# Reworking the tail, the layer-norm rows and the conditioning gradients of a fused backward kernel

## The chip, the cores and the metric

The kernel runs on one core of one Trainium2 chip. The metric is the device time of one execution in microseconds (us). A kernel is run several times and the median is quoted.

Engine names in the profile: PE is the tensor engine (matmuls), PEld its weight loads, DVE the vector engine, ACT the scalar engine, POOL the gpsimd engine, SP the engine that issues most transfers. A name ending in q (SPq) is the sequencer of that engine, which issues and waits. DMA stands for the transfer engines. "L900" is line 900 of the kernel's source.

## The reference

The program returns the output of one block and the gradients of eight of its inputs for a given `grad_out`. The block is a spectral filter (a 2-D FFT, a product with a complex weight, the inverse FFT) followed by a bilinear gated MLP; both are preceded by a layer norm that is scaled and shifted by a conditioning vector `c`. S = 2048 rows, D = 576, F = 4608, all in bf16.

```python
def _A_ref(x, w_r, w_i):                    # spectral filter
    X = rfft2(x.astype(float32)) * (w_r + 1j * w_i)
    return irfft2(X).astype(bfloat16)
def _B_ref(x, w_gate, w_up, w_down):        # gated MLP
    return ((x @ w_gate) * (x @ w_up)) @ w_down

mod = (silu(c) @ w_mod).reshape(1, 6, 1, D)
sa, ca, ga, sb, cb, gb = mod[:, 0], ..., mod[:, 5]
h = layernorm(x) * (1 + ca) + sa
x = x + ga * _A_ref(h, w_r, w_i)
h = layernorm(x) * (1 + cb) + sb
x = x + gb * _B_ref(h, w_gate, w_up, w_down)
# ... out, vjp = jax.vjp(f, A_x, w_r, w_i, w_gate, w_up, w_down, c, w_mod); vjp(grad_out)
```

The gradient of `w_mod` (576 x 3456) is the outer product of `silu(c)` with six gradient rows, those of sa, ca, ga, sb, cb, gb. The gradient of `c` (576 numbers) is `w_mod` times these six rows, times the slope of silu.

## The kernel before

The order of PE's instructions is the program's order. A list of closures called `fill` holds matmul work that is needed later but not now; `fill.run(2.5)` issues some 2.5 us of it where PE would otherwise wait. The phases are:

1. start and forward pass (to about 280 us);
2. the main loop over 18 weight blocks (to 1206.5 us), which the change does not touch;
3. **layer-norm rows**: the backward pass of the second layer norm, 16 groups of 128 rows, with the weight gradients of the last two blocks as filler;
4. **inverse transform**: eight frequency steps, with pieces of y = h·w_down (recomputed for the output; nine matmuls a piece) as filler;
5. **last rows**: 16 row groups of the first layer norm's backward pass, with the other y pieces as filler;
6. **tail**: the last two conditioning gradients, and the gradient of `c`.

The layer-norm rows. PE sums products over rows by diagonal blocks, and one filler in this stage takes its accumulator banks in pairs:

```python
def gwd(p, fb, b0):                       # gradient of w_down, 128 of its rows
    ... mm(bank[:, b0 + h, 0:288], sf[:, 0, fb, j, :], go[:, j, 288*h:288*h+288], j == 0, j == 15)   # L765
    ... # two DVE products read the pair of banks (L773)
def gw_block(p, w, m, so):                # gradient of w_gate / w_up
    ... mm(bank[:, st["b"], 0:256], h2p[...], sf[...], j == 0, False)   # L785, L789
    ... ac.copy(so()[:, m, :], bank[:, st["b"], 0:256])                 # L790, ACT frees the bank

for j in range(16):
    gh2_block(pl, j)                      # last product of the main loop, added to f32 acc on DVE
sring = [0, 1]                            # single banks;  gwd uses the pair (6, 7)
for j in range(16):
    load1(nx, ..., j + 2); load1(yl, ..., y_d, j + 2)     # row loads, 144 KB each
    n = nx[j]
    ts(n, n, rstd2[j], nmr2[j], MUL, ADD)                 # DVE
    ac.copy(b, acc[:, j, :])                              # f32 -> bf16 on ACT
    ln_bwd(b, n, mod[SCB], rstd2[j], gn, t2, go[:, j], gx)    # DVE products, ACT sums
    ...
    fill.run(1.5 if j else 4.0)
    diag_sums(b, n, j, 2, 3, 0, 192)      # of row j itself
    diag_sums(gx, yl[j], j, 5, 3, 64, None)
    fill.run(1.4)
    ...                                   # stage A of the transform of row j, ACT eviction
    if j == 11: ...                       # four table loads
for i in range(4): ...                    # w_down, 5.2 MB, after the rows
fill.flush()
```

The sums of a row group over its 128 rows are taken by ten matmuls whose diagonals are read at the end:

```python
def diag_sums(a, b, j, b0, b1, c1, col):
    for m, (d0, n) in enumerate(CH):      # four chunks of 128 columns and one of 64
        if col is not None:
            mm(bank[0:n, b1, col+m:col+m+1], a[:, d0:d0+n], ones[:, 0:1], ...)   # L898: sum of a
        mm(bank[:, b0, 128*m:128*m+128], a[:, d0:d0+n], b[:, d0:d0+n], ...)      # L900: diagonal = sum of a*b
        # m == 4: 64 columns, L902
```

The last rows and the tail:

```python
for j in range(17):
    if j < 16: Hs[j] = stage_bi(j, ...)
    if j:
        ...
        ln_bwd(gh, n, mod[SCA], ..., t2)
        fill.run(2.5)
        diag_sums(gh, n, jj, 6, 7, 0, 64)
    fill.run(2.5)
    if j in (3, 6, 9, 12): mod_grad(s, row)     # four of the six conditioning gradients
fill.flush()
diag_rows(6, 7, 0, mod[SCA], ...)               # read the diagonals, spread as rows
col_rows(7, 64, mod[SSA], ...)
mod_grad(SCA, ...); mod_grad(SSA, ...)          # the last two, 12 pairs of DVE instructions (L1130, L1131)
tensor_reduce(gc5, gsc); tt(gcb, gc5, dsl_col, MUL)
sp.dma_start(out_7[0, :].rearrange("(m q) -> q m", q=96), gcb[0:96, 0:6])   # L1174: 576 single elements
```

Of the kernel before, what the change touches and what calls it, by code (L numbers as in the profile page):

```python
# [10 lines left out]
FP32 = mybir.dt.float32  # L11
# [70 lines left out]
def build(ctx, tc, A_x, A_w_r, A_w_i, B_w_gate, B_w_up, B_w_down, c_in, w_mod, grad_out,  # L82
# [64 lines left out]
    sc_col, dsl_col, gbcol = small[:, 0:6], small[:, 6:12], small[:, 13:18]  # L147
    rstd1, nmr1 = small[:, 18:34], small[:, 34:50]
    rstd2, nmr2 = small[:, 50:66], small[:, 66:82]
    c_f, sig, tmp5 = small[:, 82:88], small[:, 88:94], small[:, 94:100]  # L150
    nt = small[:, 100:108]
    smallb = V(8640, [32])
    c_bf, sc_bf, gb_bf = smallb[:, 0:6], smallb[:, 6:12], smallb[:, 12:17]
# [52 lines left out]
    with tc.manual_schedule(engines={PE}):  # L206
# [11 lines left out]
        ve.memset(ones[:], 1.0)  # L218

# [28 lines left out]
        ve.tensor_copy(sc_col[q96], sc_bf[q96])  # L248
        ts(tmp5[q96], sig[q96], -1.0, 1.0, MUL, ADD)
        tt(tmp5[q96], tmp5[q96], c_f[q96], MUL)  # L250
        ts(tmp5[q96], tmp5[q96], 1.0, None, ADD)
        tt(dsl_col[q96], tmp5[q96], sig[q96], MUL)
# [13 lines left out]
        def mod_rows(s):  # L266
            bias = 1.0 if s in (SCA, SCB) else 0.0
            for h in range(2):
                b = single()
                for m in range(6):  # L270
                    mm(bank[:, b, 0:288], sc_rep[0:96, m, :], wm_t[s][0:96, m, 288 * h:288 * h + 288], m == 0, m == 5)
                dst = mod[:, s, 288 * h:288 * h + 288]
                if h == 0:
                    act(dst, bank[:, b, 0:288], ACT.Copy, bias=bias)
                elif bias:
                    ts(dst, bank[:, b, 0:288], bias, None, ADD)
                else:
                    ve.tensor_copy(dst, bank[:, b, 0:288])

# [261 lines left out]
        for jg in range(4):  # L541
            go_transposes(jg)
        fill.run(7.0)
# [234 lines left out]

        def gw_block(p, w, m, so):
# [36 lines left out]
        def grads(p, dring):  # L816

            out = []
            for fb in range(2):
                out += gwd(p, fb, dring())  # L820
# [15 lines left out]

        def gh2_block(p, j):
            b0 = dbank()
            for h in range(2):
                hs = slice(288 * h, 288 * h + 288)  # L840
                o = bank[:, b0 + h, 0:288]
                cs = slice(128 * j, 128 * j + 128)
                mm(o, xT[:, 1, 0, cs], wT[p][:, 0, 0, hs], True, False)  # L843
                mm(o, xT[:, 2, 0, cs], wT[p][:, 0, 1, hs], False, False)  # L844
                mm(o, xT[:, 1, 1, cs], wT[p][:, 1, 0, hs], False, False)  # L845
                mm(o, xT[:, 2, 1, cs], wT[p][:, 1, 1, hs], False, True)  # L846
# [4 lines left out]
            else:  # L851
                tt(dst, dst, src, ADD)  # L852

# [21 lines left out]
        for j in range(16):  # L875
            gh2_block(pl, j)
        nx_r = Ring(span(ST, 3, 1152), [D])
        yl_r = Ring(span(ST + 3456, 3, 1152), [D])
        F_r = Ring(span(ST + 6912, 3, 1152), [D])
        tb_r = Ring(span(ST + 10368, 2, 1152), [D])  # L880
        tg_r = Ring(span(ST + 12672, 2, 1152), [D])
        t2_r = Ring(span(ST + 14976, 2, 1152), [D])
        gx_r = Ring(span(ST + 17280, 2, 1152), [D])
        junk = V(ST + 19584, [D])
        s_r = Ring([8704, 8736], [8], FP32)
        sring = [0, 1]
        fill = Fill()
        for p in (pl - 1, pl):
            for c, f in grads(p, lambda: 6):
                fill.add(c, f)  # L890

# [12 lines left out]
        def ln_bwd(a, n, opc, rs, gn, t2, res, out):  # L904
            s = s_r.next()
            tt(gn[:], a[:], opc, MUL)  # L906
            act(junk[:], gn[:], ACT.Copy, accum_out=s[:, 0:1])  # L907
            tt(t2[:], gn[:], n[:], MUL)
            act(junk[:], t2[:], ACT.Copy, accum_out=s[:, 1:2])  # L909
            ts(s[:, 2:4], s[:, 0:2], rs, -1.0 / D, MUL, MUL)  # L910
            ts(gn[:], gn[:], rs, s[:, 2:3], MUL, ADD)  # L911
            ts(t2[:], n[:], s[:, 3:4], None, MUL)
            tt(gn[:], gn[:], t2[:], ADD)
            tt(out[:], gn[:], res, ADD)

        nx, yl = {}, {}

# [4 lines left out]
        for j in range(2):  # L922
            load1(nx, nx_r, x1_d, j, sp)
            load1(yl, yl_r, y_d, j, sp)
        for j in range(16):
            if j + 2 < 16:
                load1(nx, nx_r, x1_d, j + 2, sp)
                load1(yl, yl_r, y_d, j + 2, sp)
            n = nx[j]
            ts(n[:], n[:], rstd2[:, j:j + 1], nmr2[:, j:j + 1], MUL, ADD)  # L930
            b = tb_r.next()
            ac.copy(b[:], acc[:, j, :])
            gn, t2, gx, Fj = tg_r.next(), t2_r.next(), gx_r.next(), F_r.next()
            ln_bwd(b, n, mod[:, SCB, :], rstd2[:, j:j + 1], gn, t2, go[:, j, :], gx)
            sp.dma_start(gx1_d[:, j, :], gx[:])
            tt(gn[:], gx[:], mod[:, SGA, :], MUL)
            fold(Fj.unsqueeze(1), gn.unsqueeze(1), 1)
            fill.run(1.5 if j else 4.0)
            diag_sums(b, n, j, 2, 3, 0, 192)
            diag_sums(gx, yl[j], j, 5, 3, 64, None)  # L940
            fill.run(1.4)
            sbank[0] += 1
            ab = sring[sbank[0] % 2]
            for m in range(4):
                mm(bank[:, ab, 128 * m:128 * m + 128], Fj[:, FB[m]:FB[m] + 128], bdf, True, True)
            jj = j % 4
            mm(bank[0:32, 4, 128 * jj:128 * jj + 128], Fj[:, 256:288], bdf, True, True)
            mm(bank[32:64, 4, 128 * jj:128 * jj + 128], Fj[:, 544:576], bdf, True, True)
            evac_a(ac, ab, j)
            if jj == 3:  # L950
                evac_rem(ac, 4, j - 3, 4)
            if j == 11:
                sp.dma_start(TB.rearrange("p a b -> p (a b)"), tabs["TB"][:, :])
                sp.dma_start(TC.rearrange("p a b c -> p (a b c)"), tabs["TC"][:, :])
                sp.dma_start(TI.rearrange("p a b c -> p (a b c)"), tabs["TI"][:, :])
                sp.dma_start(TBI.rearrange("p a b -> p (a b)"), tabs["TBI"][:, :])
        wdr = V(ST + 21504, [2 * NP, D])
        for i in range(4):
            sp.dma_start(wdr[:, 9 * i:9 * i + 9, :], B_w_down[1152 * i:1152 * i + 1152, :].rearrange("(j f) d -> f j d", f=128))
        fill.flush()  # L960


        hl_t = [V(o, [NP, 256]) for o in (ACC + 24224 + 32, GO, GO + 9216, ST + 66048, ST + 75264)]
        hls = {}

        def load_hl(k):
            jp, half = k // 2, k % 2
            hls[k] = hl_t[k % 5]
            sp.dma_start(hls[k][:], hh_d[jp // 2, :, 18 * half:18 * half + 18, 256 * (jp % 2):256 * (jp % 2) + 256])

        for k in range(5):
            load_hl(k)
        RA, RB = ST, ST + 84480
        z_r = Ring(span(RA, 2, U), [4, FP])
        X_r = Ring(span(RA + 2 * U, 2, U), [2, 2, FP])
        W_r = Ring(span(RA + 4 * U, 2, U), [2, 2, FP])
        P1, P2 = V(RA + 6 * U, [2, 2, FP]), V(RA + 7 * U, [2, 2, FP])
        yb_r = Ring([ST + 62976, RA + 8 * U], [D])
        xo_r = Ring([ST + 64128, RA + 8 * U + 1152], [D])
        ac_r = Ring([RB], [2, FP], FP32)  # L980
# [252 lines left out]
```

## Time and profile before

The median of before is 1569.63 us over 13 runs (1564.67 to 1571.12). The profiled execution has a span of 1567.9 us.

| stage | from to (us) | length | PE waits in it |
|---|---|---|---|
| start, forward, main loop | 0 to 1206.54 | 1206.5 | mostly in the first 80 us |
| layer-norm rows | 1206.54 to 1317.22 | 110.68 | 17.0 |
| inverse transform | 1317.22 to 1423.55 | 106.33 | 6.4 |
| last rows | 1423.55 to 1532.23 | 108.68 | 1.3 |
| tail (after the last filler) | 1532.23 to 1567.9 | 35.67 | all |

The borders are read from PE's timeline: the end of the last gate/up group, the first matmul of the inverse transform, the first of the last rows, and the end of the last y piece.

The page of the profile, before. First the span and PE's busy time, then 40 equal slices of 39.2 us: a digit is PE's busy share in tenths, or the transfer engines'.

```profile
span 1567.9 us, 28400 instructions
PE 1475.7 (94%) x11245; PEld 988.2 (63%) x11268; DVE 810.5 (52%) x1800; ACT 515.2 (33%) x1017; POOL 261.9 (17%) x380
PE   7799998999999999999999999999999888999991
DMA  9665786976558548547745844764664598567931
```

PE is the bound (94%), and the slices show where it is not: the first ones, an eight at the end of the forward pass, three eights for the layer-norm rows and the start of the inverse transform, and the last slice, where it does almost nothing.

PE's waits from 1206 to 1318 us, before. Columns: the waiting line, what it waited for, us in total, number of times, the longest.

```profile
PE bank L785 <- ACT arena L790: 6.9, 8, 1.6
PE bank L765 <- DVE arena L773: 4.5, 2, 3.0
PE bank L785 <- ACT arena L811: 2.3, 1, 2.3
PE bank L900 <- DVE arena L914: 1.7, 2, 1.1
```

The first three are filler matmuls waiting for a bank that another engine has not emptied yet, 13.7 us together. The fourth is a row's sums waiting for that row's own chain on DVE.

Busy time in a stretch inside this stage, before. Columns: the stretch, its length, then busy us (and count) of PE, PEld, DVE, ACT and POOL, the granted clock, DMA share and GB/s.

```profile
1228.00:1270.00 42.00, 36.19 (x388) 29.33 (x388) 26.79 (x72) 21.83 (x53) 6.54 (x8) 1.00 0.89 226
```

None of the engines is full in this stretch: the rows are bound by waits among them.

The timeline of the tail, before. Columns: start, duration, engine, line, operation, out<-in; a bracket gives the idle time before it and what ended it.

```profile
1528.76 3.47 PE L1032 MATMUL bank<-arena 128*128 128x288 bf16 x27
...
1549.26 0.75 DVE L1131 SCALAR_TENSOR_TENSOR arena<-arena 96x576 bf16<-96x576 bf16 x1
...
1550.05 0.19 DVE L1170 TENSOR_REDUCE arena<-arena 128x6 f32<-128x36 f32 x1
1550.27 0.16 DVE L1172 TENSOR_TENSOR arena<-arena 96x6 bf16<-96x6 f32 x1
1550.46 0.32 SPq L1174 DMA_DIRECT2D out_dram<-arena  x1
```

The transfers issued between 1530 and 1568 us, before: how many, KB each, median us from issue to landing.

```profile
out_dram<-arena SPq DMA_DIRECT2D x2, 648.0 KB, 7.7
out_dram<-arena SPq DMA_DIRECT2D x3, 144.0 KB, 1.7
out_dram<-arena SPq DMA_DIRECT2D x1, 1.1 KB, 16.1
```

PE's last filler ends at 1528.76 + 3.47 = 1532.23. DVE then works until 1550.4, with only short pieces of PE and ACT beside it, and then a store of 1.1 KB takes 16.1 us, while a 144 KB store takes 1.7. No engine computes beside it. The packets in the profile, those of this store and of a 648 KB store before it, are over at 1553.5 us; from then to the landing at 1566.6 us the profile shows none. What the store waits for in these 13 us is not shown.

In the last rows, the sums of one row group are these PE lines of the timeline, before (the other eight of the ten alternate between these two kinds, the last pair with 64 columns):

```profile
1430.95 0.17 PE L898 MATMUL bank<-arena 128*128 128x1 bf16 x1
1430.98 0.22 PE L900 MATMUL bank<-arena 128*128 128x128 bf16 x1
...
1431.55 2.38 PE L1032 MATMUL bank<-arena 128*128 128x288 bf16 x18
```

From the first to the next filler matmul they hold PE for 0.60 us.

### The profile page before, as it was taken

The numbers are of one execution on the slowest core, as the hardware profiler recorded it, in microseconds if no ns is written. First come the engines' busy times: TensorE is split into PE (matmuls) and PEld (weight loads), VectorE is DVE, ScalarE is ACT, GpSimd is POOL, SyncE is SP. The second block draws the span as 40 slices with busy tenths as digits, with TensorE's granted clock in tenths as the row PEclk, the third lists the DMA queues.
The fourth block names the chain that finished last, engine by engine and source line by source line (L and its number), as shares of the span: only waits on it lengthen the run. The fifth ranks groups of instructions, "written<-read, shape, count | busy, mean of one in ns | idle before, by whom it ended". The sixth has DMA issues, their size and how long they took to land. (4 is left out here: it accounts for less than half of the span.)

```text
span 1567.9 us, 28400 instructions
## 1 busy us (share of the span) xinstructions
PE 1475.7 (94%) x11245; PEld 988.2 (63%) x11268; DVE 810.5 (52%) x1800; ACT 515.2 (33%) x1017; POOL 261.9 (17%) x380
## 2 busy tenths in 40 slices
PE   7799998999999999999999999999999888999991
PEld 4344443576677668667667766866766666676770
DVE  6424486533543443353354344335337775778864
ACT  5666675212212221221221222122033344343431
POOL 1122421212112202211211220221110110000000
PEclk9899998999999999999999999999999999999995
DMA  9665786976558548547745844764664598567931
GB/s 273 189 147 156 204 233 166 190 159 163 120 114 186 128 97 167 139 116 138 163 124 112 186 127 97 167 137 116 141 148 107 158 263 232 156 184 209 277 111 46
DMA packets 440998, 248.76 MB, mean 159 GB/s; under 512 B 318048, under 2 KB 418336, under 8 KB 440352
## 3 DMA queue, kind: packets, MB, share of 16 engines
q1 hardware_dynamic: 418256, 177.19, 50.4%
q0 software_dynamic: 22464, 69.62, 14.8%
q8 instruction: 88, 1.44, 0.4%
q14 instruction: 46, 0.38, 0.1%
q10 hardware_dynamic: 144, 0.13, 0.0%
HBM read 96.90 MB, written 74.20 MB: 109 GB/s over the span
## 5 line engine op out<-in xcount | busy, mean ns | idle before, releaser
L852 DVE TENSOR_TENSOR arena<-arena,bank 128x576 f32<-128x576 f32 x272 | 204.9, 753 | 305.2 <-PE bank L846 305.2
L740 ACT CAST arena<-bank 128x512 bf16<-128x512 f32 x144 | 84.4, 586 | 391.1 <-PE bank L730 373.6
L846 PE MATMUL bank<-arena 128*128 128x288 bf16 x576 | 164.6, 286 | 0.0
L843 PE MATMUL bank<-arena 128*128 128x288 bf16 x576 | 163.9, 285 | 0.5 <-DVE arena L850 0.2
L845 PE MATMUL bank<-arena 128*128 128x288 bf16 x576 | 164.3, 285 | 0.0
L844 PE MATMUL bank<-arena 128*128 128x288 bf16 x576 | 164.1, 285 | 0.0
L785 PE MATMUL bank<-arena 128*128 128x256 bf16 x1152 | 149.5, 273 | 9.2 <-ACT arena L790 6.9
L1032 PE MATMUL bank<-arena 128*128 128x288 bf16 x1152 | 152.4, 287 | 0.0
L765 PE MATMUL bank<-arena 128*128 128x288 bf16 x1152 | 146.7, 288 | 4.5 <-DVE arena L773 4.5
L734 PE MATMUL bank<-arena 128*128 128x512 bf16 x576 | 149.9, 383 | 1.0 <-ACT arena L740 1.0
L789 PE MATMUL bank<-arena 128*128 128x256 bf16 x1152 | 149.4, 273 | 0.0
L736 PE MATMUL bank<-arena 128*128 128x512 bf16 x576 | 148.7, 381 | 0.0
L765 PEld LDWEIGHTS <-arena 128*128 128x128 bf16 x1152 | 112.7, 98 | 36.7 <-issue 4.7
L1032 PEld LDWEIGHTS <-arena 128*128 128x128 bf16 x1152 | 110.8, 98 | 31.7 <-issue 3.2
L785 PEld LDWEIGHTS <-arena 128*128 128x128 bf16 x1152 | 111.0, 98 | 25.8 <-issue 12.8
L789 PEld LDWEIGHTS <-arena 128*128 128x128 bf16 x1152 | 111.9, 98 | 13.3
L744 DVE TENSOR_TENSOR arena<-arena 128x512 bf16<-128x512 bf16 x144 | 61.2, 425 | 107.3 <-ACT arena L740 107.3
L790 ACT CAST arena<-bank 128x256 bf16<-128x256 f32 x144 | 53.5, 371 | 184.1 <-PE bank L789 184.1
L734 PEld LDWEIGHTS <-arena 128*128 128x128 bf16 x576 | 50.6, 98 | 80.2 <-issue 33.0
L736 PEld LDWEIGHTS <-arena 128*128 128x128 bf16 x576 | 56.6, 98 | 68.7 <-issue 1.3
L741 ACT CAST arena<-bank 128x512 bf16<-128x512 f32 x144 | 84.8, 589 | 23.9 <-PE bank L736 23.3
L321 ACT CAST arena<-bank 128x1024 bf16<-128x1024 f32 x72 | 72.7, 1010 | 56.8 <-PE bank L317 29.1
(217 smaller groups left out, 2206.2 us busy)
## 6 DMA issues: line engine op xcount, KB each, us to landing
ghh_d<-arena POOLq DMA_DIRECT2D x72, 256.0 KB, 3.5
arena<-ghh_d POOLq DMA_DIRECT2D x36, 512.0 KB, 5.8
hh_d<-arena SPq DMA_DIRECT2D x36, 512.0 KB, 4.5
arena<-hh_d SPq DMA_DIRECT2D x16, 1152.0 KB, 7.4
out_dram<-arena POOLq DMA_DIRECT2D x36, 256.0 KB, 5.1
arena<-in_B_w_down_dram POOLq DMA_DIRECT2D x18, 288.0 KB, 4.2
out_dram<-arena POOLq DMA_DIRECT2D x36, 144.0 KB, 5.5
arena<-in_B_w_down_dram SPq DMA_DIRECT2D x4, 1296.0 KB, 7.8
```

The lines of the kernel that those rows point to most:

```text
L734: mm(bank[:, bg, :], w[:, m, fs], h2T[:, js, m, :], odd == 0 and m == 0, odd == 1 and m == 3)
L736: mm(bank[:, bu, :], w[:, 4 + k, fs], h2T[:, js, m, :], odd == 0 and k == 0, odd == 1 and k == 3)
L741: ac.copy(u[:], bank[:, bu, :])
L765: mm(bank[:, b0 + h, 0:288], sf[:, 0, fb, j, :], go[:, j, 288 * h:288 * h + 288], j == 0, j == 15)
L785: mm(bank[:, st["b"], 0:256], h2p[:, j, 128 * m:128 * m + 128], sf[:, 1 + w, :, j, :], j == 0, False)
L789: mm(bank[:, st["b"], 0:256], h2p[:, j, 128 * m:128 * m + 128], sf[:, 1 + w, :, j, :], False, j == 15)
L843: mm(o, xT[:, 1, 0, cs], wT[p][:, 0, 0, hs], True, False)
L844: mm(o, xT[:, 2, 0, cs], wT[p][:, 0, 1, hs], False, False)
L845: mm(o, xT[:, 1, 1, cs], wT[p][:, 1, 0, hs], False, False)
L846: mm(o, xT[:, 2, 1, cs], wT[p][:, 1, 1, hs], False, True)
L852: tt(dst, dst, src, ADD)
L1032: mm(bank[:, yb, 0:288], hl[:, fb % 18, 128 * (j % 2):128 * (j % 2) + 128], wdr[:, fb, 288 * h:288 * h + 288], fb == 0, fb == 35)
```

## The change

Its intent is to take PE's waits out of the last 360 us:

1. **Tail.** The last two conditioning rows come out of the sums directly as rows. Their part of the gradient of `c` is done by 45 one-column matmuls with a transposed load of `w_mod`. The gradient of `c` is turned into a row by five small matmuls and stored as one run of 1152 bytes.
2. **Last rows.** Ten diagonal-sum matmuls per row group become four column-sum matmuls of 64 columns. The other four conditioning gradients are done on 128 partitions.
3. **Layer-norm rows.** Five single banks rotate. The last product is written as bf16, so ACT's cast is gone. Two DVE operations of a row become ACT operations. The sums and stage A of row j are issued two rows later. Some filler is held back for the inverse transform, w_down is loaded during the rows (2.7 MB of it in row 12), and all masks come in one lump at the end.
4. **Inverse transform.** The filter's gradients are one step later, and there is more filler ahead of the last part of a step.
5. **Start.** silu(c) in the columns that parts 1 and 2 need comes from four small element-wise loads of `c`.

The diff, cut to its core:

```diff
+        po.memset(c2_bf[:], 0.0)                                   # start
+            for h in range(2):
+                po.dma_start(c2_bf[64 * h:64 * h + 64, 0:9], c_in[0, :].rearrange("(m q) -> q m", q=64))
+            po.dma_start(c2_bf[:, 9:13], ...); po.dma_start(c2_bf[0:64, 13:14], ...)
@@ layer-norm rows
-        for j in range(16):
-            gh2_block(pl, j)
-        sring = [0, 1]
+        sring = [0, 1, 4, 6, 7]
-            for c, f in grads(p, lambda: 6):
+            for c, f in grads(p):                                  # gwd_halves: single banks
+        def gh2_last(j):
+                tt(acc_b(j)[:, hs], acc[:, j, hs], bank[:, b, 0:288], ADD)      # bf16 out
-            ts(n[:], n[:], rstd2[:, j:j + 1], nmr2[:, j:j + 1], MUL, ADD)
-            ac.copy(b[:], acc[:, j, :])
+            act(n[:], n[:], ACT.Identity, bias=nmr2[:, j:j + 1], scale=rstd2[:, j:j + 1])
-            ts(gn[:], gn[:], rs, s[:, 2:3], MUL, ADD)
-            ts(t2[:], n[:], s[:, 3:4], None, MUL)
+            act(t2[:], n[:], ACT.Identity, bias=s[:, 2:3], scale=s[:, 3:4])
+            ts(gn[:], gn[:], rs, None, MUL)
+            if fill.left() > 9.0: fill.run(1.0)
+            if 2 <= j < 18: row_sums(j - 2)
+            if fill.left() > 9.0: fill.run(1.0)
+            if 2 <= j < 18: row_a(j - 2)
+            if j == 12: load_wdr(9, 28)
+            if j == 14: ...                                        # four table loads
+        load_wdr(28, 36)
@@ inverse transform
-                fill.run(4.0)
+                fill.run(5.0)
                 stage_ci(u, Y_t, SD_t, Gt)
-                gws[u] = grad_W(u, X)
@@ last rows
-                diag_sums(gh, n, jj, 6, 7, 0, 64)
+            if j: column_sums([gh, q], 6, j - 1, 64)
+        def column_sums(srcs, b, j, w):
+            for h in range(2):
+                for i, a in enumerate(srcs):
+                    mm(bank[w*i:w*i+w, b+h, 0:288], ones[:, 0:w], a[:, 288*h:288*h+288], ...)
@@ tail
-        diag_rows(...); col_rows(...); mod_grad(SCA, ...); mod_grad(SSA, ...)
-            sp.dma_start(out_7[0, :].rearrange("(m q) -> q m", q=96), gcb[0:96, 0:6])
+        fill.run(4.0)
+        ...                                                        # row -> columns, nine outer products, stores
+        fill.run(4.0)
+        for m in range(5):
+            for i in range(9):
+                mm(bank[0:n, 2, m:m + 1], wmT[:, i, 128*m:128*m+n], dmc[:, i:i + 1], i == 0, i == 8)
+        ...
+        for m in range(5):
+            mm(bank[0:1, m // 4, ...], gcb[0:n, m:m + 1], ident[0:n, 0:n], True, True)
+        ac.dma_start(out_7[0:1, :], grow[0:1, :])
```

## The prediction

> **What bounds it now.** The tensor engine, with three exceptions. The page has PE busy 1475.7 of 1567.9 us (94%), DVE 52%, ACT 33%. The table by stretches puts PE's idle time in three places: about 20 us in the first 80 us (start-up, DMA share near 1.0); about 25 us between 1206 and 1532 (layer-norm rows 17 us, inverse transform 7 us, last rows 1 us); and everything after 1532. The 980 us of the main loop hold almost none, and the instruction order there is unchanged.
>
> **The tail.** In the timeline PE's last filler group ends near 1532.2. DVE then does the last layer-norm row, two mask/row steps and twelve pairs of 0.37 and 0.75 us (last conditioning gradients) until 1550.4. The last store, 1.1 KB as 576 two-byte elements, is issued at 1550.46 and takes 16.1 us to land; the synchronising engine waits for it. That is 35.7 us after PE's last work. The Trainium skill, "DMA: Bandwidth & Descriptors" (Specifications), says transfers under 512 B make the DMA read-modify-write; 16.1 us against 1.7 us for 144 KB stores in the same window agrees. The change does the two late gradients by some 45 one-column matmuls (the trace issues such ones every 0.05 to 0.08 us), writes the row from one partition, and keeps a little PE filler for the waits. Row copy, small copies, matmuls, product, transposition, a 2 us store and the end, chained: about 12 to 13 us. Gain: 23 us, all critical.
>
> **Last rows.** Per row PE does 5.0 us of filler, 0.97 us transform and 0.62 us diagonal sums (6.64 us a row, PE full). Four half-width matmuls replace ten; paired 64-column matmuls already in this trace (16 of 256 columns in about 1.0 us) show pairs overlapping, so 0.25 to 0.3 us. Gain: 16 x 0.35 = 5.6 us. DVE falls from about 6.7 to 5 us a row and stays under PE.
>
> **Layer-norm rows.** PE waits here for ACT evictions of single banks (6.9 + 2.3 us), for DVE double-bank evictions (4.5) and row chains (2). The change uses five rotating single banks, sums and transforms two rows behind, and saves the 0.67 us accumulator cast per row; the last product is written as bf16 directly. My sums per row afterwards: PE 3.8 us, DVE 3.2, ACT 3.3, so PE should bind. I expect PE idle here to fall from 17 to about 6 us. Against it, all masks now run in one lump before the inverse transform with filler held behind it: +3 us of PE idle. Inverse transform: about 2 us better from the longer filler before its last step. Net gain about 10 us.
>
> **Added at the start.** 1,728 two-byte elements through four POOL-issued loads in a window where the DMA share is 1.0; their cast stands on DVE ahead of the copy that the first evictions wait for (8.1 us now). Estimate: +2 us, anywhere from 0 to 6.
>
> **Sum:** 1569 - 23 - 5.6 - 10 + 2, with a little unmodelled slack in the rows, is about 1530 us; range 1513 to 1546. Faster by over 2%: 0.75; within: 0.24; slower: 0.01.
>
> **Right if:** the stretch from PE's last filler to the end is 10 to 15 us and the last store lands in about 2 us; last rows take about 6.3 us each; the layer-norm stage shows PE idle well under 10 us with no large wait on single-bank evictions; the first eviction of the start is at most a few us later.
>
> **Wrong if:** DVE/ACT ping-pong per row, in the order fixed by the scheduler, exceeds 4 us a row, so PE starves with five banks full; the late 2.8 MB weight load delays the tables that the inverse transform needs; the tiny start loads hold DVE for over 5 us; or the mask lump costs 6 us or more.

## The result, and the profile after

The changed kernel has a median of 1528.99 us over 8 runs (1526.89 to 1531.74). The ratio to before is 0.9745, with a 95% interval of 0.9735 to 0.9755. A ratio is the mean time of one kernel's fast runs over that of the other's of the same rounds, so it is not quite the ratio of the medians quoted.

The page, after (slices of 38.2 us):

```profile
span 1526.9 us, 28365 instructions
PE 1469.7 (96%) x11213; PEld 982.6 (64%) x11236; DVE 782.3 (51%) x1734; ACT 558.9 (37%) x1065; POOL 266.0 (17%) x388
PE   6799999899999999999999999999999998899997
DMA  9755697894485475566466566568548369888872
```

PE's busy time has hardly moved (1475.7 to 1469.7 us). Of the 41 us, 35.0 are waits (92.2 us before, 57.2 after) and 6.0 are busy time: the last slice reads 7 in place of 1. But two eights are left, where the DMA line reads 9 and 8.

| stage | before | after | difference | filler moved | net |
|---|---|---|---|---|---|
| to the end of the main loop | 1206.54 | 1208.40 | +1.86 | | +1.9 |
| layer-norm rows, masks | 110.68 | 84.45 | -26.23 | 10.5 us out | -15.7 |
| inverse transform | 106.33 | 113.36 | +7.03 | 10.5 us in, 3 y pieces (3.4 us) out | -0.1 |
| last rows | 108.68 | 110.41 | +1.73 | 3 y pieces in | -1.6 |
| tail | 35.67 | 10.28 | -25.39 | | -25.4 |
| span | 1567.9 | 1526.9 | -41.0 | | |

The column "net" removes filler that only changed its place. 10.5 us are the twelve half-blocks held back, as the timeline has them. A y piece takes 1.12 us (45 matmuls in 5.6 us); 55 of the 128 are in the inverse transform before, 52 after. Not in the column: the last two reversals of filter gradients, some 0.5 us of matmuls, also moved from the inverse transform to the last rows.

PE's waits in the rows, 1208 to 1293 us, after:

```profile
PE bank L971 <- DMA arena<-y_d: 4.0, 2, 2.8
PE bank L828 <- ACT arena L833: 0.8, 1, 0.8
PE bank L1153 <- ACT arena L1154: 0.7, 1, 0.7
PE bank L1153 <- ACT arena L412: 0.6, 1, 0.6
```

The 13.7 us of waits for filler banks have become 0.8. The largest wait is a new one: a row load of y has not landed. The last two lines (L1153 is the matmul that spreads a mask as rows) are the price of the mask lump, 1.3 us.

The stretch inside this stage, after:

```profile
1228.00:1270.00 42.00, 41.17 (x471) 33.39 (x470) 39.36 (x115) 38.05 (x91) 7.72 (x9) 1.00 0.77 188
```

PE has become full here (36.19 to 41.17 us of 42), and DVE (39.36) and ACT (38.05) have almost no room below it.

The inverse transform, after: PE's largest wait there, and then a table of stretches of the same kernel.

```profile
PE bank L468 <- DMA arena<-in_A_w_r_dram: 5.2, 1, 5.2
```

```profile
1300.00:1310.00 10.00, 6.10 (x33) 4.19 (x34) 1.08 (x3) 2.32 (x4) 0.78 (x1) 0.66 1.11 279
```

L468 reverses a tile of the spectral filter, and the tile's load had not landed. The DMA share is 1.11 at that moment. The granted clock is 0.66 in the mean of these 10 us: in finer windows it is 1.00 until 1301.7, 3.2 us into the wait, and 0.50 from 1301.8 to 1308.6, so PE works at half clock from the end of the wait at 1303.79 for 4.8 us more. The Trainium skill, "TensorE: Matmul & The Clock Gate" (Part 1), says that the tensor engine's clock is halved after an idle window of about 3.4 us. This wait of 5.2 us fits, but shorter ones did it too: in before the clock is 0.50 from 1412.8 to 1416.2 after a wait of 1.98 us, the longest since 1317. Before has 6.8 us at 0.50 in its inverse transform as well (the other half from 1317.2 to 1320.6), and both kernels have 0.97 in the mean of this stage, so the lower clock is no difference between them.

The tail's timeline, after:

```profile
1515.34 1.28 PE L1025 MATMUL bank<-arena 128*128 128x288 bf16 x9
...
1518.11 1.29 PE L1340 MATMUL bank<-arena 128*128 128x1 bf16 x40 [0.53 <-DVE arena L1327]
...
1519.85 0.50 PE L1347 MATMUL bank<-arena 128*1 128x128 bf16 x5 [0.45 <-DVE arena L1343]
1520.27 0.68 DVE L1348 CAST arena<-bank 1x512 bf16<-1x512 f32 x1 [0.41 <-PE bank L1347]
...
1521.03 0.53 ACTq L1350 DMA_DIRECT2D out_dram<-arena  x1
```

The transfers issued between 1512 and 1527 us, after:

```profile
out_dram<-arena SPq DMA_DIRECT2D x6, 216.0 KB, 3.4
out_dram<-arena SPq DMA_DIRECT2D x2, 144.0 KB, 2.5
```

From PE's last filler to the last store's issue it is now 4.4 us (1516.62 to 1521.03), before it was 18.2. From that issue to the end of the span it is 5.9 us, before 17.4. The landing of the last store has no figure of its own in this view, but the only two packets of its queue move between 1522 and 1523 us, within 2 us of its issue, while packets of the 216 KB stores, issued until 1522.97, run to 1525.4. So these ordinary stores of the gradient of `w_mod`, and no longer the store of the gradient of `c`, are what lands last.

The sums of one row group in the last rows, after: the four half-width matmuls and the next instruction.

```profile
1435.89 0.44 PE L979 MATMUL bank<-arena 128*64 128x288 bf16 x4
1436.26 0.42 PE L524 MATMUL bank<-arena 128*128 128x288 bf16 x2
```

From start to start they hold PE for 0.37 us, in place of 0.60.

At the start, the tiny loads delay one cast on DVE. One line of the timeline, after:

```profile
11.35 0.17 DVE L285 CAST arena<-arena 128x14 f32<-128x14 bf16 x1 [5.83 <-DMA arena<-in_c_dram]
```

DVE stood 5.83 us for them. The first eviction that the forward pass waits for starts at 12.50 us, before at 9.11.

### The profile page after: what moved, and what is told of

It is laid out like the page before. It is cut to its first block, busy times and chain, and to the rows that moved or that the text cites. A ratio compares the mean times of both kernels' runs of the same rounds, so it can differ in the third digit from the quotient of the medians.

```text
span 1526.9 us, 28365 instructions
## 1 busy us (share of the span) xinstructions
PE 1469.7 (96%) x11213; PEld 982.6 (64%) x11236; DVE 782.3 (51%) x1734; ACT 558.9 (37%) x1065; POOL 266.0 (17%) x388
## 5 line engine op out<-in xcount | busy, mean ns | idle before, releaser
L901 DVE TENSOR_TENSOR arena<-arena,bank 128x576 f32<-128x576 f32 x256 | 192.9, 754 | 305.2 <-PE bank L890 305.2
L890 PE MATMUL bank<-arena 128*128 128x288 bf16 x576 | 164.6, 286 | 0.0
L889 PE MATMUL bank<-arena 128*128 128x288 bf16 x576 | 164.3, 285 | 0.0
L887 PE MATMUL bank<-arena 128*128 128x288 bf16 x576 | 164.0, 285 | 0.2 <-DVE arena L899 0.2
L888 PE MATMUL bank<-arena 128*128 128x288 bf16 x576 | 164.1, 285 | 0.0
L1025 PE MATMUL bank<-arena 128*128 128x288 bf16 x1152 | 148.6, 286 | 0.0
L1025 PEld LDWEIGHTS <-arena 128*128 128x128 bf16 x1152 | 111.4, 98 | 31.0 <-issue 3.1
L781 PE MATMUL bank<-arena 128*128 128x288 bf16 x1024 | 128.1, 286 | 0.0
L828 PEld LDWEIGHTS <-arena 128*128 128x128 bf16 x1152 | 110.8, 98 | 17.8 <-issue 4.7
L832 PEld LDWEIGHTS <-arena 128*128 128x128 bf16 x1152 | 112.8, 98 | 14.2 <-issue 0.4
L781 PEld LDWEIGHTS <-arena 128*128 128x128 bf16 x1024 | 100.2, 98 | 28.2
L760 DVE TENSOR_TENSOR arena<-arena 128x512 bf16<-128x512 bf16 x144 | 61.2, 425 | 107.4 <-ACT arena L756 107.4
L750 PEld LDWEIGHTS <-arena 128*128 128x128 bf16 x576 | 50.5, 98 | 80.1 <-issue 32.9
L752 PEld LDWEIGHTS <-arena 128*128 128x128 bf16 x576 | 56.6, 98 | 68.6 <-issue 1.1
```

Source lines behind the costliest of these rows:

```text
L750: mm(bank[:, bg, :], w[:, m, fs], h2T[:, js, m, :], odd == 0 and m == 0, odd == 1 and m == 3)
L752: mm(bank[:, bu, :], w[:, 4 + k, fs], h2T[:, js, m, :], odd == 0 and k == 0, odd == 1 and k == 3)
L781: mm(bank[:, b0 + h, 0:288], sf[:, 0, fb, j, :], go[:, j, 288 * h:288 * h + 288], j == 0, j == 15)
L828: mm(bank[:, st["b"], 0:256], h2p[:, j, 128 * m:128 * m + 128], sf[:, 1 + w, :, j, :], j == 0, False)
L832: mm(bank[:, st["b"], 0:256], h2p[:, j, 128 * m:128 * m + 128], sf[:, 1 + w, :, j, :], False, j == 15)
L887: mm(o, xT[:, 1, 0, cs], wT[p][:, 0, 0, hs], True, False)
```

## The experiments

Twelve kernels were run in three calls. Each call ran on its own chip with its own runs of before (medians 1566.99, 1569.29 and 1567.31 us), so a kernel is compared with the changed one by ratios to before. "Against the changed kernel" is (ratio - 0.9745) x 1568 us; both intervals together leave an uncertainty of some 2.6 us, for e6 to e9 of some 3.8 us. All were correct.

| run | us (median) | ratio, 95% interval | against the changed kernel |
|---|---|---|---|
| e1_element_store | 1540.19 | 0.9826 [0.9812, 0.984] | +12.7 |
| e2_late_grads_dve | 1532.29 | 0.9775 [0.9762, 0.9788] | +4.7 |
| e3_before_row_store | 1555.36 | 0.9922 [0.9909, 0.9936] | (-12.2 against before) |
| e4_double_sums | 1531.01 | 0.9768 [0.9754, 0.9782] | +3.6, intervals just overlap |
| e6_two_filler_banks | 1528.03 | 0.9737 [0.9715, 0.9759] | -1.3, within the scatter |
| e7_no_row_lag | 1532.32 | 0.9754 [0.9733, 0.9775] | +1.4, within the scatter |
| e8_filter_first | 1526.22 | 0.9728 [0.9706, 0.975] | -2.7, intervals overlap |
| e9_weights_spread | 1525.43 | 0.9717 [0.9695, 0.9738] | -4.4, intervals just overlap |
| e10_three_loads_moved | 1523.0 | 0.9719 [0.9704, 0.9734] | -4.1 |
| e5b_cast_after | 1527.57 | 0.9748 [0.9734, 0.9761] | +0.5, within the scatter |
| e11_banks_of_before | 1529.37 | 0.9758 [0.9745, 0.9772] | +2.0, intervals overlap |
| e12_row_chain_before | 1529.27 | 0.9757 [0.9744, 0.9771] | +1.9, intervals overlap |

How far does a stage repeat? Five profiled executions have the rows and the inverse transform as in the changed kernel (the changed kernel itself, e1, e2, e4 and e5b): the rows last 84.5 to 86.1 us, the inverse transform 111.3 to 113.4 us, and PE's waits in the rows are 3.7 to 5.1 us for DMA and 2.1 to 2.8 us for other engines. Before and e3 differ only in the last store, yet their rows last 110.7 and 113.3 us. One source shows in the granted clock, which drops to 0.50 in pieces of 3.4 us: one piece in before's rows, four in e3's. So the length of a stage in one profile is good to some 2 to 3 us, no better.

The theory was that of the prediction: the tail's gain is mostly the element-wise store and the DVE chain before it; the last rows gain by shorter sums on a full PE; the layer-norm rows gain by banks that come free in time. The rivals were: the store hides behind other stores, so removing it gains little; half-width matmuls do not overlap; and it is not the banks but the lag of two rows, or the shifted operations, that makes the rows faster.

### e1: the changed kernel, storing the gradient of c by elements

```diff
-        grow = ...                                   # five matmuls, two copies
-        ac.dma_start(out_7[0:1, :], grow[0:1, :])
+            ac.dma_start(out_7[0, 0:512].rearrange("(m q) -> q m", q=128), gcb[:, 0:4])
+            ac.dma_start(out_7[0, 512:576].rearrange("(m q) -> q m", q=64), gcb[0:64, 4:5])
```

> The changed kernel with one thing undone: the last 1.1 KB gradient goes out as 2-byte elements from columns again (two stores, no transposition into a row). Theory (the store of 576 elements is on the end of the chain): its landing goes from about 2 us to 14-16 us, and the kernel is 11 to 14 us slower than the changed one (1529), so about 1541. Rival (other stores of the tail end at nearly the same time, or the gain came from the arithmetic alone): at most 4 us slower.

Measured: 12.7 us slower than the changed kernel; the tail is 21.84 us, not 10.28. The transfers issued between 1510 and 1537 us, e1:

```profile
out_dram<-arena SPq DMA_DIRECT2D x6, 216.0 KB, 15.3
...
out_dram<-arena ACTq DMA_DIRECT2D x1, 1.0 KB, 15.7
out_dram<-arena ACTq DMA_DIRECT2D x1, 0.1 KB, 15.7
```

The theory held. What was not expected is the first line: the six ordinary stores of 216 KB, issued by another engine, landed after 15.3 us, not 3.4. The Trainium skill, "DMA: Bandwidth & Descriptors" ("Issuing engines are not separate DMA queues"), says that transfers of all issuing engines run on the same 16 engines and interleave. That allows a slowdown but does not explain this one. The queues in the same window (27 us), e1: packets, MB, share of 16 engines; q1 has the ordinary stores, q10 the element-wise ones.

```profile
q1 hardware_dynamic: 1536, 1.62, 69.0%
q10 hardware_dynamic: 608, 0.00, 1.7%
```

And q1 in the 15 us from 1512 to 1527, after:

```profile
q1 hardware_dynamic: 1536, 1.62, 38.8%
```

The element-wise packets took little of the engines' time, but the same 1536 ordinary packets took 3.2 times as much (69.0% of 27 us against 38.8% of 15 us). An element-wise store also holds up the stores around it; by what mechanism is not shown.

### e3: before, with the row store alone

```diff
-            sp.dma_start(out_7[0, :].rearrange("(m q) -> q m", q=96), gcb[0:96, 0:6])
+        for m in range(6):
+            mm(bank[0:1, m // 5, 96*(m % 5):96*(m % 5) + 96], gcb[0:96, m:m + 1], ident[0:96, 0:96], True, True)
+        ve.tensor_copy(grow[0:1, 0:480], ...); ac.copy(grow[0:1, 480:576], ...)
+        sp.dma_start(out_7[0:1, :], grow[0:1, :])
```

> The kernel before, with one part of the change alone: its last gradient is turned into a row by six small matmuls and stored as one 1152-byte row. Theory: the last landing falls from 16 to about 2 us, and two copies and six matmuls add about 1.5 us: 11 to 14 us faster than before, about 1556.5. Rival as for the first run: under 4 us.

Measured: 12.2 us faster than before; the tail falls from 35.67 to 22.42 us. Adding the part alone and taking it away (e1) give the same 12 to 13 us, so this one store is half of the tail's 25.4 us, in either kernel.

### e2: the changed kernel, with the last two gradients on DVE

```diff
-        for i in range(5): ... mm(..., R2[0:1, ...], ones[0:1, 0:1], True, True)     # row to columns
-        ...
-        for m in range(5):
-            for i in range(9): mm(bank[0:n, 2, m:m+1], wmT[...], dmc[:, i:i+1], i == 0, i == 8)
+        for k in range(3):
+            for i in range(3):
+                ve.scalar_tensor_tensor(out=pr_t, in0=wk[:, i, :], scalar=1.0, in1=R2, ..., accum_out=gsc3[...])
+                ts(wk[:, i, :], R2[:], sc64[:, m:m + 1], None, MUL)
+        mm(bank[0:64, 2, 0:5], fold_f[:], gsc3[:, 0:9:2], True, True); ...
```

> The changed kernel with the late conditioning gradient (shift and scale rows) done by the vector engine again: nine pairs of a multiply-accumulate (0.75 us) and a scaling (0.37 us) on 128 partitions after the last row sums, in place of 45 one-column matmuls; row store kept. Theory: the chain grows by about 9.5 us of vector work less the 3 to 4 us it replaces, so 5 to 8 us slower than the changed kernel, about 1535. Rival (that work hides under the kept filler and the last stores): under 2 us.

Measured: 4.7 us slower; the tail is 14.87 us, 4.6 more. So doing this part by small matmuls gives nearly 5 us, a little under the 5 to 8 us expected. The edit also puts on DVE the three scalings that ACT does in the changed kernel; they are part of this price.

e1 and e2 account for about 17 of the tail's 25.4 us. If the parts simply add up, the other 8 us belong to what neither undoes: rows that come directly out of the sums, two gradients at once on 128 partitions, and filler kept for the last row's chain. They were not taken apart.

### e4: the changed kernel, with every column sum taken twice

```diff
+            for rep in range(2):
                 for h in range(2):
                     for i, a in enumerate(srcs):
-                        mm(..., j == 0, j == 15, ...)
+                        mm(..., j == 0 and rep == 0, j == 15 and rep == 1, ...)
-        ac.copy(halves(R2), bank[:, 6:8, 0:288])
+        act(halves(R2), bank[:, 6:8, 0:288], ACT.Copy, scale=0.5)
```

> The changed kernel with every half-width column-sum matmul of the last rows done twice and the sums halved on eviction (same result). It prices the matmuls that replaced the ten diagonal-sum ones. If PE is the bound of the last rows, as I hold, the kernel slows by 16 times the price of four such matmuls: 16 x 0.37 = 5.9 us if their cost is what the trace of the changed kernel shows from start to start, 16 x 0.25 = 4.0 us if pairs overlap as the prediction had it. If the vector or scalar engine bounds those rows, under 1 us.

Measured: 3.6 us slower, and the last rows are 113.89 us long, not 110.41. One row group's sums, e4:

```profile
1435.94 0.68 PE L980 MATMUL bank<-arena 128*64 128x288 bf16 x8
1436.55 0.42 PE L524 MATMUL bank<-arena 128*128 128x288 bf16 x2
```

Eight take 0.61 us from start to start, four take 0.37. So four more cost 0.24 us, and 16 x 0.24 = 3.8 us appear in the stage (3.5) and in the time (3.6, with an uncertainty of some 2.7): PE is the bound of this stage. 0.24 us is also what two full-width matmuls of 288 columns take here (18 in about 2.21 us from start to start, 0.12 each). So two half-width ones run side by side, as the Trainium skill, "TensorE: Matmul & The Clock Gate" (Part 3, "Packing small matmuls"), has it. The first four cost 0.37 - 0.24 = 0.13 us more: probably an entry or exit cost of such a group, for which that page has no figure.

### e6: the changed kernel, with two banks for the rows' filler

```diff
-        sring = [0, 1, 4, 6, 7]                 # during the rows
+        sring = [0, 1]                          # filler; set after the last products, which keep five banks
+        rring = [4, 6, 7]                       # stage A of the rows
```

> The changed kernel with the filler matmuls of the layer-norm rows kept to two accumulator banks (0 and 1), the row transforms on 4, 6, 7; everything else stays. Theory (five rotating banks took away PE's waits on single-bank evictions, 9 us in the kernel before): waits on the filler's evictions come back, 5 to 9 us slower than the changed kernel, which stands at a ratio of 0.9745 to before; so about 0.979. Rival (the lighter row chain did it, the banks are incidental): within 2 us of the changed kernel.

Measured: no change in time. The rows are 83.81 us long, 84.45 in the changed kernel. In this form the theory of the banks fell: filler does not need five. It still had single banks only, and stage A had three of its own. Therefore e11 below.

### e7: the changed kernel, without the lag of two rows

```diff
-            if 2 <= j < 18: row_sums(j - 2)
+            if j < 16: row_sums(j)
-            if 2 <= j < 18: row_a(j - 2)
+            if j < 16: row_a(j)
```

> The changed kernel with the sums and the transform of a layer-norm row emitted in the same step as the row, not two rows behind. Theory: with vector and scalar engine each above 90% busy, and PE also full, the two-row lag is what lets PE run on: without it PE waits for the vector engine's row chain at each row, 4 to 10 us slower. Rival (the vector engine runs ahead by its own rings, so the order on PE matters little): under 2 us.

Measured: the time cannot be told apart from that of the changed kernel (+1.4 us). The rows are 98.05 us long, 12 to 13.6 us more than in the five executions of the same code, and the inverse transform is 106.41 us long, 5 to 7 us less. In the rows PE waited 11.9 us, once, for a row load of y, and 3.8 us for DVE. So the lag hides the rows' chain, but its larger effect is that it hides late row loads. Much of what was lost came back: PE does not wait for the filter tile at all here (5.2 us in the changed kernel), since the transfers that the later stage needs had that much more time to land.

### e8: the changed kernel, loading the filter before the rest of w_down

```diff
+        W_r = Ring(span(ST + 4 * U, 2, U), [2, 2, FP])
+        for u in range(2): Ws[u] = W_r.next(); load_W(sp, Ws[u], u)
         load_wdr(28, 36)
         ...
-        for u in range(2): Ws[u] = W_r.next(); load_W(sp, Ws[u], u)
```

> The changed kernel with the loads of the first two filter tiles issued before the last weight load and the first two hidden-state loads, rather than behind them. Theory (in the changed kernel PE stood 5.2 us for such a tile, behind 3.5 MB in the same queue): this wait goes; 3 to 6 us faster, ratio about 0.9715. Rival (the queue is full anyway, something else then arrives late): under 1.5 us, with a wait of like size elsewhere.

Measured: 2.7 us less by the ratio, not beyond the scatter. The wait of 5.2 us for the filter tile is gone from PE's waits. In its place PE waits 4.6 us for DVE, in the same stage, at L507, where it waited 1.2 us in the changed kernel. The stage is 111.1 us long, no clear difference from the 111.3 to 113.4 us of the same code.

### e9: the changed kernel, with the 2.7 MB load of row 12 in three parts

```diff
-            if j == 12: load_wdr(9, 28)
+            if j in (1, 5, 10):
+                load_wdr(*{1: (9, 13), 5: (13, 20), 10: (20, 27)}[j])
-        load_wdr(28, 36)
+        load_wdr(27, 36)
```

> The changed kernel with the 2.7 MB weight load of row 12 split into three that go out at rows 1, 5 and 10, as soon as the buffers under them are read. Theory (row loads and row stores queued behind the 2.7 MB: PE waited 4.0 us for row loads, the vector engine 4.8 us for a row store): those waits go, and the filter tile lands earlier too; 3 to 7 us faster, ratio about 0.9715. Rival: the bytes are the same and the waits only move; under 1.5 us.

Measured: 4.4 us less by the ratio and 3.3 by the span; the intervals touch. PE's waits for DMA in rows and inverse transform fall from 9.2 us (9.0 to 10.5 in the five executions of the same code) to 6.0 us. The large load ahead of the others in the queue does cost some of the row loads' and the filter's time.

### e10: the two together, and the tiny loads of c later

```diff
 # e8 and e9 (the parts of w_down end at 27, then the filter, then the rest), and at the start:
-        po.memset(c2_bf[:], 0.0)
-        ...                                  # the four loads
-        silu_columns()
 # after the conditioning rows of the forward pass are computed:
+        po.tensor_scalar(out=c2_bf[:], in0=mod[:, SGB, 0:14], scalar1=0.0, ..., op0=MUL)   # zero, once these rows exist
+        ...                                  # the four loads
+        silu_columns()
```

> The changed kernel with three moves of loads: the filter tiles first, the 2.7 MB weight load spread over three rows, and the 2-byte start loads held until the forward transform. Theory: PE's DMA waits between 1270 and 1310 (9 us in the changed kernel) fall under 3 us and the start shift of 1.85 us goes; 7 to 10 us faster than the changed kernel, ratio about 0.969. Rival (the queue is full for 60 us and the waits only move): under 4 us.

Measured: 1523.0 us, ratio 0.9719. It has the lowest median and is about 4 us (0.26%) below the changed kernel, with intervals just apart; by the ratio e9 (0.9717) is as fast, so against e9 it gained nothing more. The main loop starts at 250.4 us, 1.4 us earlier than in the changed kernel; that is within the scatter given under e5b. PE's waits for DMA fell further, to 4.4 us, but its other waits in the inverse transform rose from 2.8 to 6.0 us. PE's largest wait there, and the DVE line behind it, e10:

```profile
PE bank L450 <- DVE arena L435: 5.3, 2, 4.6
```

```profile
1311.13 0.76 DVE L1172 SCALAR_TENSOR_TENSOR arena<-arena 128x576 bf16<-128x576 bf16 x1 [8.50 <-DMA arena<-in_w_mod_dram]
```

L1172 is a conditioning gradient that nobody needs soon. It stood 8.50 us for its own load of `w_mod`, in front of the step (L435) that PE needed. The rival, that waits move instead of going away, was right for 3.2 of the 4.8 us: that much of what PE no longer waited for DMA, it waited for other engines.

### e5b: the changed kernel, with the tiny loads and their cast later at the start

```diff
 # the four loads of c, their memset and the cast stand later in the program, where e10 has them;
 # unlike in e10, no instruction was put in to make the loads themselves wait
```

> The changed kernel with the same 2-byte start loads at the same time, but with the cast of them behind, not ahead of, the copy that the first evictions need. In the trace of the changed kernel the main loop starts 1.85 us later than before. Theory (the cast held the vector engine for 5.8 us, that is the shift): the first evictions start 2 to 3 us earlier, the main loop 1 to 2 us earlier. Rival (the traffic of the tiny loads delays the large loads that the start waits for): the main loop starts within 0.5 us of the changed kernel's. The trace decides; the time is near the noise.

Measured: nothing that can be told apart. The first eviction came at 9.4 us, not 12.5, but the cast then waited until 16.3 us and the first filler matmul came at 22.5 us (21.1 in the changed kernel). The edit did not keep the loads where they were: POOL issued two of the four only at 8.42 us, after a wait for DVE, where the changed kernel has issued all four by 4.3 us. The main loop starts at 250.2 us, in the changed kernel at 251.8; the other kernels with the change's start lie between 250.1 and 252.0, and the two with before's start at 249.9 (before) and 247.8 (e3). Inconclusive.

### e11: the changed kernel, with the bank plan of before in the rows

```diff
-        sring = [0, 1, 4, 6, 7]
+        sring = [0, 1]                          # shared by filler and stage A
-                b = sbk(); stage_a_rem(..., b, i); evac_rem(ac, b, ...)
+                stage_a_rem(..., 4, i); evac_rem(ac, 4, ...)
```

> The changed kernel with the accumulator banks of the layer-norm rows as in the kernel before: filler and row transforms share banks 0 and 1, the remainder has bank 4. Giving filler two banks of its own (earlier run) cost nothing. If sharing with the transforms was what made PE wait on single-bank evictions before, the row stage slows by 5 to 9 us; if the lighter row chain did it, under 2 us.

Measured: +2.0 us, intervals overlap. PE's waits in the rows other than for DMA rise from 2.1 us (2.1 to 2.8 in the five executions of the same code) to 6.1 us, e11:

```profile
PE bank L394 <- DVE arena L814: 1.9, 1, 1.9
PE bank L806 <- DVE arena L814: 1.6, 2, 1.0
```

These are waits for banks: stage A (L394) and filler (L806) for a bank that DVE has not read out. In the stretch 1228 to 1270 us PE is busy for 37.06 us, close to before's 36.19. But the wait of 4.0 us for y is gone, since the loads had more time, and the rows, 85.9 us, are no longer than the 84.5 to 86.1 us of the changed rows. The wait for the filter tile is 7.3 us in place of 5.2. The pair of banks that before gave to one filler was put back by no run.

### e12: the changed kernel, with the row's operations on DVE as before

```diff
-            act(n[:], n[:], ACT.Identity, bias=nmr2[...], scale=rstd2[...])
+            ts(n[:], n[:], rstd2[...], nmr2[...], MUL, ADD)
-            ln_bwd_b(nx[j], gn, t2, ...)
+            ...                                  # as ln_bwd of before, on DVE
```

> The changed kernel with three operations of each layer-norm row back on the vector engine (the normalisation and both scalings, about 0.6 us a row more there and 1.2 us a row less on the scalar engine), banks and lag as changed. The vector engine is 95% busy in these rows. If the moved operations are what let PE run full, the row stage slows by 4 to 8 us; if the banks or the lag did it, under 2 us.

Measured: +1.9 us, intervals overlap. (The edit moves two operations from ACT to DVE; the third, one of the scalings, was on DVE already and gets its second operand back.) DVE is busy for 41.55 us of the same 42 us (39.36 in the changed kernel), and PE waits for it, e12:

```profile
PE bank L971 <- DVE arena L1056: 4.9, 3, 3.1
```

Waits other than for DMA rise to 7.0 us. Again the wait of 4.0 us for y is gone in exchange, and the rows (85.81 us) are no longer than the same code has them elsewhere.

## Why the prediction was right, point by point

The time was predicted as 1530 us and measured as 1528.99. The terms of the sum were less exact than the sum.

| term | predicted | measured | shown by |
|---|---|---|---|
| start | +2 | +1.9 at the end of the main loop, scatter about 2 | stages; e5b could not separate it |
| layer-norm rows, mask lump, inverse transform | -10 | -15.7 and -0.1, so -15.8 | stages and waits; e7, e11, e12 |
| last rows | -5.6 | -1.6 | stages; e4 |
| tail | -23 | -25.4 | stages; e1, e2, e3 |
| sum | -36.6, and some 2.4 of slack | -41.0 | |

**Tail: right in cause, 2.4 us too small.** The stretch from PE's last filler to the end was to be 10 to 15 us and is 10.28. The element-wise store is 12 to 13 us of it (e1, e3), the small matmuls 4.7 (e2). The Trainium skill's statement in "DMA: Bandwidth & Descriptors" (Specifications), that below 512 bytes the DMA reads, modifies and writes, names the kind of transfer; its cost comes from the traces: 16.1 us for 576 elements, 13 of them without a packet in the profile, so that reading and writing back is what costs the time is not shown. That the store now lands in about 2 us agrees with its packets, which move within 2 us of its issue; the 5.9 us from its issue to the end belong to the ordinary stores.

**Layer-norm rows: the waits fell as predicted, the gain was larger, and which part of the change brings it is not shown.** "PE idle here to fall from 17 to about 6 us": the waits fell from 17.0 to 6.1 us, but 4.0 of the 6.1 are for the row loads of y, which the prediction did not name (2.1 are other), so the close match is partly luck. The stage's net gain of 15.7 us is larger than these 10.9 us. The predicted +3 us for the mask lump was 1.3 us of waits. The rest is in PE's busy time. The whole stage in the table of stretches, before:

```profile
1206.54:1317.22 110.68, 93.53 (x921) 73.53 (x920) 81.48 (x211) 51.93 (x127) 13.67 (x20) 0.98 0.85 233
```

And after:

```profile
1208.40:1292.85 84.45, 78.32 (x825) 62.57 (x823) 71.87 (x207) 60.68 (x132) 13.30 (x19) 0.98 0.84 238
```

The counts differ by 96 matmuls, which are the twelve half-blocks of eight that were held back, worth 10.5 us. PE's busy time fell by 15.2. So much the same other matmuls held PE for 4.7 us less, which the prediction did not count, at the same clock of 0.98. A matmul behind a wait shows its whole duration (a mean of 0.29 us for L846) as busy, one in a stream about 0.12; fewer interruptions would give such a drop, but no run tests that. e11 and e12 show that the banks and the shifted operations each remove some 4 to 5 us of PE's waits for other engines, and e6 that two banks for filler are enough if stage A has its own and no pair is used. Neither costs its 4 to 5 us in time when it is undone alone. Below it lies the second bound: late row loads, whose wait of 4.0 us disappears as soon as PE is later. No run that undoes one part (e6, e7, e11, e12) brings back more than 2 us of the 15.7, each with an uncertainty of some 3 us. The single banks in place of a pair and the bf16 output of the last product, which saves the cast, were not undone alone. So how the 15.7 us divide among the parts stays open.

**Inverse transform: wrong, by 2 us.** "About 2 us better from the longer filler" was 0.1. PE's waits for DVE in this stage fell from 6.4 to 2.8 us, those before the last part of a step from 3.7 (L492) to 1.2 (L507), so the step "longer filler before its last step" did what it should; but 5.2 us of waiting for the filter tile took its place, which the sum had not counted. The prediction's own warning, that the late weight load could delay what this stage needs, came true for the filter and the row loads, not for the tables that it named. With other orders and sizes of the loads that wait goes (e8) or shrinks to 3.5 us (e9); what this gains in time is at the edge of the scatter.

**Last rows: the term that was mis-sized.** "So 0.25 to 0.3 us. Gain: 16 x 0.35 = 5.6 us." The direction and the bound were right (e4: PE is full, pairs overlap). But four half-width matmuls in a group hold PE for 0.37 us, 0.13 us more than their bare 0.24, and the diagonal sums took 0.60, not 0.62. That gives 16 x 0.23 = 3.7 us. The stage as measured has 16 of the new groups and, by its border, only 15 of the old; 15 x 0.60 - 16 x 0.37 = 3.1. The last two reversals of filter gradients were moved into this stage, at about 0.5 us (an estimate: four matmuls of about 290 columns at the 0.12 us of the y matmuls). 2.6 us of gain remain against 1.6 measured; 1 us is within the scatter of a stage between executions (e3, whose last rows are those of before, has 107.4 us for 108.7) and stays open.

**Start: right in size.** The tiny loads delay the first eviction by 3.4 us and the end of the main loop by 1.9 us. Runs with the same start scatter by about 2 us where the main loop starts (250.1 to 252.0 with the change's start, 249.9 and 247.8 with before's), so no more than the sign and the order of size is shown.

**The prediction's own signs.** The tail, PE's waits in the rows and the first eviction are as its "right if" says. A last row takes 6.9 us in the mean (110.41 / 16), not 6.3; 0.2 of that are the three y pieces that moved in. One of its "wrong if" signs did come: the tiny loads held DVE for 5.83 us, over 5; it cost no more than the +2 us of the sum.

The errors of the single terms mostly cancelled: the last rows and the inverse transform gave some 6 us less than predicted (4 and 2), the layer-norm rows with the masks and the tail some 10 us more (8 and 2). That the sum came within 1 us is therefore partly luck.

## What to carry to other kernels

Read the end of the program first: a tiny store whose elements lie on different partitions cost 12 to 13 us here, a third of the whole gain, and five small matmuls that make it a row removed it. Where PE is almost full, count a change by waits removed and matmuls saved in its own stage, and take filler that only moved out of the comparison. When one part is undone and the time stays, look at the waits before calling the part worthless: here a second bound, the transfer queue, took up what the first gave back, and reordering its loads moved waits to other engines as well as removing some.

## What the Trainium skill lacked or had wrong

- "DMA: Bandwidth & Descriptors" gives 512 bytes as the smallest transfer for line rate, but no price for an element-wise store. In these runs 576 two-byte elements took 16.1 us to land (15.7 in e1) and 12 to 13 us of kernel time; 144 KB took 1.7 us. In before, 13 of the 16.1 us passed with no packet in the profile.
- The same page says that transfers of all issuing engines interleave, but not how much a tiny element-wise store slows ordinary ones: 216 KB stores landed after 15.3 us beside it (e1) and after 3.4 us without.
- "TensorE: Matmul & The Clock Gate" (Part 3) gives the overlap of packed matmuls, which the runs confirm (four more half-width ones in 0.24 us), but no cost of starting such a group between full-width matmuls, and "TensorEngine Tiling (Array Packing)", which says that a change of the tiling mode drains the engine, has no time for it either: about 0.13 us here (0.37 us for the first four).
- "TensorE: Matmul & The Clock Gate" (Part 1) gives an idle window of about 3.4 us before the clock is halved. In these traces shorter waits were enough: the clock is 0.50 from 1412.8 to 1416.2 us in before after a wait of 1.98 us, and from 1289.9 to 1293.2 us in e9 after waits of 0.98 and 0.63 us and into one of 0.73 us. How much idle time within which stretch decides it, the runs do not show.
